# A decode kernel of two interleaved layers: two P buffers, half a V unit more kept on chip, and wq's space as ring slots

## The chip, the cores and the metric

The kernel runs on one core of a Trainium2 chip. The core has a matrix engine (TensorE, PE in the profile), a vector engine (VectorE, DVE), an activation engine (ScalarE, ACT), GpSimd (POOL, used for a little setup only) and SyncE (SP), which here does nothing but issue DMAs and wait. The engines run their own instruction streams in order and meet through semaphores. SBUF is the on-chip memory of 128 partitions, PSUM the accumulators that TensorE writes. The metric is the device time in microseconds (us), as the median of several runs; lower is better.

## The reference

Two rounds of the same pair of layers, on a batch of four rows with one token each. Both rounds use the same weights and the same K and V caches, so every cache byte that isn't kept on chip is read twice.

```
B, D, Hq, Hkv, Sk, Dh, F = 4, 512, 32, 8, 8192, 128, 1792
def A(x):                      # grouped-query attention on a cache
    q = (x @ wq) as (B, Hq, 1, Dh)           # 4 query heads share a K/V head
    p = softmax(q @ k_cache.T * Dh**-0.5)
    return (p @ v_cache) as (B, 1, Hq*Dh) @ wo
def Bf(x):                     # feed-forward network (FFN)
    return (silu(x @ w_gate) * (x @ w_up)) @ w_down
x = A_x
x = x + A(layernorm(x));  x = x + Bf(layernorm(x))      # "layer 0"
x = x + A(layernorm(x));  x = x + Bf(layernorm(x))      # "layer 1"
```

All tensors are bf16. K and V caches are 4 x 8 x 8192 x 128 each, 134 MB together, and the four rows are independent of each other up to the end.

## The kernel before, in words

**Units.** The caches are read in units of 4096 positions of one row `b` and one K/V head ("group" `g`): 1 MiB, 8 KB in each of 128 partitions. There are two units (`cp` 0 and 1) to a group, eight groups to a row, four rows, two layers `l`: 128 units of K and 128 of V. A unit lies in one of ten slots of a ring in SBUF (`pool`, `NSLOT`), each with a semaphore of its own; a unit has two halves of 2048 positions.

**K.** VectorE transposes both halves in place in 32 x 32 blocks (`k_pair`, L576, 1.2 us each). TensorE multiplies them with the padded query (L588) into four PSUM banks that hold the scores of a whole row. When all 16 units of a row have been added, `softmax` takes the maxima (L606), the exponentials into one of the buffers of `pp` (the "P buffer", L610), a common maximum for each query head (L620 to L649), and transposes P (L665, L671). A pass of a row is ready 18 to 22 us after its last K unit landed.

**V.** `v_group` multiplies P with the two units of a group (`pv4`, L744), folds the four column groups together on VectorE (L763, L766), turns the result (L772) and scales it into `oT` (L781). `oproj` (L707) multiplies a group's part of `oT` with wo; in layer 0 it follows each group of each row, and in layer 1 it follows the groups of row 3 alone, for all four rows at once. The very last V group of the order takes a direct form (`pv1`, L730) that needs no fold.

**Between the layers.** When all eight groups of a row are through layer 0, `chain` runs that row's FFN, a LayerNorm and the projection with wq (L465, in two halves), and only then can K of layer 1 of that row be multiplied. The rows are staggered: the passes (l, b) run in the order (0,0), (0,1), (1,0), (0,2), (1,1), (0,3), (1,2), (1,3). After (1,3) there is one more FFN for all rows (`ffn`), whose result is transposed back (`fin1`, L1023), copied (`fin2`, L1030) and stored (L1038).

**What stays on chip.** Of each row five V units (groups 0 and 1, and `cp` 0 of group 2) stay in their slots from layer 0 to layer 1 (`KEPT`, `kept_of`); the load is left out in layer 1 (`vload`). 128 + 108 units and the weights make 261.4 MB.

**What sets the order.** Loads are issued by SP alone, in the order of the string `ORDER`: a letter is a K unit, a V unit, or a piece of a weight (q, o, g, u, d for wq, wo, gate, up, down). K units come in the order of the passes, V units in that of `vgroups`. Everything else is placed by a planner (`Plan`): it knows a fixed time for each step, runs the steps on model engines, gives each load the slot that has been free longest (`pump`), picks at each point the ready step with the lowest priority number, and then the program is emitted in order of the planned starts. So the order on each engine, and which load goes into which slot, are fixed when the kernel is built. A V step's priority is the place of its load in `ORDER`; a unit that is kept takes the place of the load before it.

**What sets the waits.** `_Sync` keeps for every named piece of memory the last writer and the readers since. An instruction that reads a name waits for its last writer; one that writes a name waits for its last writer and all readers. For a DMA the writer's mark is its semaphore with all 16 signals, that is, its landing:

```
for w in writes:
    rec = self.res.get(w)
    if rec is not None:
        add(rec.w)
        for sv in rec.r.values():
            add(sv)
```

SP's waits (L62) stand in its queue, so what is behind a waiting load isn't issued. A load waits for the readers of its slot, which are TensorE's products with the unit before.

Of the kernel before, what the change touches and what calls it, by code (L numbers as in the profile page):

```python
# [102 lines left out]
class Step:  # L103
    __slots__ = ("eng", "us", "deps", "fn", "prio", "take", "free", "start", "end", "loads", "slot_of", "pairs")

    def __init__(self, eng, us, fn, deps, prio, take=None, free=None, pairs=0):
        self.eng, self.us, self.fn, self.prio = eng, us, fn, prio
        self.pairs = pairs
        self.deps = [d for d in deps if d is not None]
        self.take, self.free = take, free  # L110
        self.start = self.end = None
        self.slot_of = None


class Plan:
# [26 lines left out]
    def run(self):  # L142
# [44 lines left out]
        def pump(now):  # L187
            nonlocal li, sp_at, dma_at
            while li < len(self.loads):
                s = self.loads[li]  # L190
                t = sp_at
                if s.slot_of is not None:
                    if not slots:
                        return
                    slots.sort()
                    f, i = slots[0]
                    t = max(t, f)
                    if t > now:
                        return
                    slots.pop(0)  # L200
                    self.slot[s.slot_of] = i
                s.start = t
                sp_at = t + 0.4
                dma_at = max(dma_at, t + self.LOAD_LEAD) + s.us
                s.end = dma_at + self.LOAD_TAIL
                li += 1
                finish(s)
# [4 lines left out]
        while left:  # L212
# [16 lines left out]
            if li < len(self.loads) and (slots or self.loads[li].slot_of is None):  # L229
                nxt = max(sp_at, min(slots)[0] if self.loads[li].slot_of is not None else 0.0)  # L230
# [20 lines left out]
            if s.slot_of is not None:  # L251
                slots.append((s.end + self.HOP, self.slot[s.slot_of]))
            left -= 1
# [5 lines left out]
    def emit(self):  # L259
        for s in sorted(self.steps + self.loads, key=lambda s: (s.start, s.prio[0])):  # L260
# [3 lines left out]
ORDER = ("qKVKKKKKKKKVKKVVKKKKVgKKKKuKgKKKoVVVVVKKKVKKKVVKKKVVVuoododVKVKVKKKKVKKKKKKKVKKKVVVKVKKKKKKKKKKV"  # L264
         "KKKKKVVVVVVVVVVVVVVVVVVVKKVKKKKKKKKKVKKKKKKVVKKVVKKKKVKVKKKKVKKKKVVVVVVVVVVVVVVVVVVKKKKKKKKKKKKK"
         "KKKVVVVVVVVVVVVVVVVKVVVVKVKKKKKKKKKKKKKKVVVVVVVVVVVVVVV")
KEPT = [5, 5, 5, 5]
NSLOT = 10
VCUT = [4, 5, 0, 3]
NTAIL = [0, 3, 4, 1]  # L270


def bass_interleave_layers__gqa_block_cached__swiglu_ffn__decode_kernel(
# [33 lines left out]
    with ExitStack() as es:  # L307
# [7 lines left out]
        pp = sb("pp", [P, 3, NCH * 512], BF16)  # L315
# [8 lines left out]
        invL = sb("invL", [P, 3, 32], FP32)  # L324
        xrow = pp[0:B, 0, 0:D]
        ones1 = sb("ones1", [P, 1], FP32)
# [14 lines left out]
        negm = sb("negm", [P, 3, 4], FP32)  # L341
        lsum = sb("lsum", [P, 3, 4], FP32)
        gm = sb("gm", [P, 1], FP32)
        gl = sb("gl", [P, 1], FP32)
        alpha = sb("alpha", [P, 3, 4], FP32)
# [7 lines left out]
        xoT = sb("xoT", [P, NQ * B], BF16)  # L353
# [14 lines left out]
        sem_slot = [sem(f"sem_slot{i}") for i in range(NSLOT)]  # L368
        sem_x = sem("sem_x")
        sem_out = sem("sem_out")  # L370
# [67 lines left out]
        def layer_norm(dep, tag):  # L438
            m = col_sum(XT, mean, "x", "mean", [dep], tag + "m")

            def center():
                op("dve", lambda e: e.tensor_tensor(xnT[:].rearrange("p (n b) -> p n b", b=B), XT[:], over_nq(mean),
                                                    ALU.subtract), reads=["x", "mean"], writes=["xnT"])
                op("dve", lambda e: e.tensor_tensor(dT[:], XT[:], over_nq(mean), ALU.subtract),
                   reads=["x", "mean"], writes=["dT"])
                op("dve", lambda e: e.tensor_tensor(sqT[:], dT[:], dT[:], ALU.mult), reads=["dT"], writes=["sqT"])
            c = PL.add("dve", 0.5, center, [m], CHAIN)
            v = col_sum(sqT, var, "sqT", "var", [c], tag + "v")
# [97 lines left out]

        def unit_ap(u, h):
            s = PL.slot[home[u]]
            return pool[:, s, h * UE:(h + 1) * UE], f"slot{s}_{h}"

        def load_pair(u):
            kind, l, b, g, cp = u

            def fn():
                s = PL.slot[home[u]]
                cache = A_k_cache if kind == "k" else A_v_cache
                src = cache[b, g, cp * 2 * CR:(cp + 1) * 2 * CR, :].rearrange("(p t) d -> p (t d)", p=P)
                T.dma("sp", pool[:, s, :], src, sem_slot[s], writes=[f"slot{s}_0", f"slot{s}_1"])
            home[u] = u
            return PL.load(2.5, fn, u)  # L560
# [3 lines left out]
        p_free = {0: None, 1: None, 2: None}  # L564
# [150 lines left out]
        def v_group(l, b, g, lds, prios):  # L715
# [4 lines left out]
            for i, cp in enumerate(VCP):  # L720
# [32 lines left out]
                if not (l == 0 and (g, cp) in kept_of[b]):  # L753
                    st.slot_of = home[u]
                prev = st
# [19 lines left out]
            if not direct:  # L775
                prev = PL.add("dve", 0.9, fold, [prev], CHAIN)
# [13 lines left out]
        def ffn_mm(w_sb, wname, deps, tag):  # L790
            def fn():
                bk = pbk(tag)
                for fo in range(FO):
                    for kt in range(KT):
# [5 lines left out]
                           sig=(kt == KT - 1 and fo == FO - 1))  # L800
            return PL.add("pe", 1.65, fn, deps + [w_load[f"{wname}0"], w_load[f"{wname}1"]], CHAIN, take=tag, pairs=KT * FO)

        def ffn(dep, tag, dst=None, dkey="x"):
            v = lambda t: t.rearrange("p (f b) -> p f b", b=B)
            cen, root = layer_norm(dep, tag + "n")
            gate = ffn_mm(wg_sb, "wg", [cen], tag + "g")
            up = ffn_mm(wu_sb, "wu", [cen, gate], tag + "u")
# [9 lines left out]
            s = PL.add("act", 0.3, a2, [s], CHAIN)  # L817

            def a3():
# [3 lines left out]
                op("dve", lambda e: e.tensor_tensor(gs[:], gs[:], eneg[:], ALU.mult), reads=["gs", "eneg"], writes=["gs"])  # L823
            s = PL.add("dve", 1.0, a3, [s], CHAIN)

            def a4():
                bk = pbk(tag + "u")
                op("dve", lambda e: e.tensor_tensor(v(eneg[:]), v(ps[:, bk * BW:bk * BW + FO * B]), rstd_fo(), ALU.mult),
                   reads=[f"pb{bk}", "rstd"], writes=["eneg"])
                op("dve", lambda e: e.tensor_tensor(hT[:], gs[:], eneg[:], ALU.mult), reads=["gs", "eneg"], writes=["hT"])  # L830
            s = PL.add("dve", 0.45, a4, [s, up], CHAIN, free=tag + "u")
# [11 lines left out]
            return add_x(XT, "x", tag + "d", [s], dst, dkey)  # L843

        def add_x(base, key, tag, deps, dst=None, dkey="x"):
            to = XT[:].rearrange("p n b -> p (n b)") if dst is None else dst

            def fn():
                bk = pbk(tag) if tag else OPJ
                op("dve", lambda e: e.tensor_tensor(to, base[:].rearrange("p n b -> p (n b)"),  # L850
                                                    ps[:, bk * BW:bk * BW + NQ * B], ALU.add),
                   reads=[key, f"pb{bk}"], writes=[dkey])
            return PL.add("dve", 0.2, fn, deps, CHAIN, free=tag)

        def chain(b, deps, prior):
# [11 lines left out]
            q_ready[(1, b)] = out_  # L867

# [20 lines left out]
        def v_first(b):  # L889
            nk = -(-KEPT[b] // NCP)  # L890
            return [g for g in range(nk, G)] + list(range(nk))

        def v_second(b):
            nk = -(-KEPT[b] // NCP)
            kept, rest = list(range(nk)), list(range(nk, G))
            r = []
            while kept or rest:
                if kept:
                    r.append(kept.pop(0))
                if rest and (len(r) < 2 * nk - 2 or not kept):  # L900
                    r.append(rest.pop(0))
            return r
        vgroups = [(0, 0, g) for g in v_first(0)]
        rest = v_first(1)
        vgroups += [(0, 1, g) for g in rest[:G - NTAIL[1]]]
        for b in range(B):
            vgroups += [(1, b, g) for g in v_second(b)[:VCUT[b]]]
            if b + 1 < B:
                vgroups += [(0, b + 1, g) for g in v_first(b + 1)[G - NTAIL[b + 1]:]]
            vgroups += [(1, b, g) for g in v_second(b)[VCUT[b]:]]  # L910
            if b + 2 < B:
                vgroups += [(0, b + 2, g) for g in v_first(b + 2)[:G - NTAIL[b + 2]]]
# [36 lines left out]
        for i, (l, b) in enumerate(KSEQ):  # L949
            pb_of[(l, b)] = b % 3  # L950
# [47 lines left out]
        pend = list(vgroups)  # L998
# [19 lines left out]
        s = ffn(s, "z", dst=xoT[:], dkey="xo")  # L1018

        def fin1():  # L1020
            bk = pbk("out")
            for nq in range(NQ):
                op("pe", lambda e: e.matmul(bank_bf(bk)[0:B, nq * P:(nq + 1) * P], lhsT=xoT[:, nq * B:(nq + 1) * B],  # L1023
                                            rhs=ident[:], is_transpose=True, start=True, stop=True),
                   reads=["xo", "ident"], writes=[f"pb{bk}"], sig=(nq == NQ - 1))
        s = PL.add("pe", 0.6, fin1, [s], CHAIN, take="out", pairs=NQ)

        def fin2():
            bk = pbk("out")
            op("dve", lambda e: e.tensor_copy(xrow, bank_bf(bk)[0:B, 0:D]), reads=[f"pb{bk}"], writes=["xrow"])  # L1030
        PL.add("dve", 0.4, fin2, [s], CHAIN, free="out")
# [6 lines left out]
        nc.sync.dma_start(out.rearrange("b s d -> (b s) d"), xrow).then_inc(sem_out, 16)  # L1038
        nc.sync.wait_ge(sem_out, 16)

# [28 lines left out]
```

## Time and profile before

| | |
|---|---|
| median of 3 runs | 654.46 us (653.19 to 657.21) |
| the profiled execution: its own time | 656.26 us |
| its span, first to last instruction | 654.4 us |
| mean granted TensorE clock | 0.645 |
| TensorE busy | 473.6 us (72%) |
| VectorE busy | 461.6 us (71%) |
| ScalarE busy | 48.4 us (7%) |
| read from HBM | 261.36 MB, 399 GB/s over the span |
| chain that ended last | DMA 56%, TensorE 24%, VectorE 14%, SP 4%, issue 2% |

The profile is of one execution, and times in it count from the span's start. Busy time leaves out semaphore and DMA-issuing instructions. Its slices divide the span into 40 equal parts of 16.4 us. A "releaser" is what an engine's wait ended on. The landing of a load is when its semaphore has all 16 signals; the trace holds each signal. With the DMA queue full, two K units land 2.49 us apart.

The last load lands at 640.4. K's last unit of row 3, layer 1, lands at 602.9, its scores end at 608.3, and its P is ready at 620.8.

### The profile page before, as it was taken

Reading aid. Unit: us, or ns where it says so; the run is one execution under the profiler, and the core shown is the slowest. Engines: PE = TensorE matmul, PEld = TensorE weight load, DVE = VectorE, ACT = ScalarE, POOL = GpSimd, SP = SyncE. Lnnn points to the kernel's source line nnn. Section 1 sums busy time; section 2 is a strip of 40 time slices with the busy share of each in tenths; the row PEclk is TensorE's granted clock in tenths of the full one; section 3 lists DMA queues with packets and bytes.
Section 4 is the critical chain, followed back from the end, with each engine's and each line's share of the span. In section 5 each row is a group of like instructions: output and inputs, shape, how many; then the busy total and the mean of one; then the engine's idle time right before and its main releaser. Section 6 shows DMA issues by size and latency. Waiting matters only on the chain.

```text
span 654.4 us, 17105 instructions
## 1 busy us (share of the span) xinstructions
PE 473.6 (72%) x7774; PEld 208.7 (32%) x7774; DVE 461.6 (71%) x822; ACT 48.4 (7%) x114; POOL 2.7 (0%) x8
## 2 busy tenths in 40 slices
PE   2565457676876787677987686777877788977697
PEld 2211123125421232245422132235421234521246
DVE  2786684764697899744698888864699645689453
ACT  1000110003000110110000110030000200000300
POOL 1000000000000000000000000000000000000000
PEclk9975687665576578755555668755577665567655
DMA  8999999999999999999999999999999999999990
GB/s 350 419 422 407 402 398 419 420 416 393 408 416 412 412 419 420 420 419 417 378 426 418 421 419 421 420 420 419 391 389 422 420 420 420 383 394 422 420 413 21
DMA packets 41673, 262.48 MB, mean 401 GB/s; under 512 B 3960, under 2 KB 9856, under 8 KB 10880
## 3 DMA queue, kind: packets, MB, share of 16 engines
q1 hardware_dynamic: 41600, 261.38, 97.7%
q8 instruction: 61, 1.00, 0.6%
q14 instruction: 12, 0.10, 0.0%
HBM read 261.36 MB, written 0.00 MB: 399 GB/s over the span
## 4 chain that ended last, share of the span: by engine, by line
DMA 56%; PE 24%; DVE 14%; SPq 4%; issue 2%; ACT 0%; DVEq 0%
DMA pool<-in_A_k_cache_dram 33%; DMA pool<-in_A_v_cache_dram 19%; DVE pool L576 8%; PE ps L744 7%; PE ps L588 7%; SPq L92 4%; DVE red L766 3%; DMA wd_sb<-in_B_w_down_dram 3%; PE ps L772 2%; PE ps L465 2%; PE ps L795 2%; PE ps L707 1%; DVE red L763 1%; PE ps L837 1%; PE ps L427 1%
## 5 line engine op out<-in xcount | busy, mean ns | idle before, releaser
L576 DVE STREAM_TRANSPOSE pool<-pool 128x1024 uint32<-128x1024 uint32 x256 | 303.2, 1222 | 57.1 <-DMA pool<-in_A_k_cache_dram 50.1
L588 PE MATMUL ps<-pool,qpad 32*32 32x512 bf16 x4096 | 238.3, 541 | 74.4 <-DVE pool L576 69.4
L588 PEld LDWEIGHTS ps<-pool,qpad 32*32 32x32 bf16 x4096 | 67.6, 108 | 222.9 <-DVE pool L576 148.0
L744 PE MATMUL ps<-pool,pp 128*32 128x512 bf16 x1008 | 112.4, 556 | 30.9 <-DMA pool<-in_A_v_cache_dram 27.7
L766 DVE SCALAR_TENSOR_TENSOR red<-ps,mask,red 128x128 f32<-128x128 f32 x189 | 66.3, 351 | 6.7
L772 PE MATMUL ps<-sel,red 128*128 128x4 f32 x126 | 33.1, 337 | 41.2 <-DVE red L766 36.3
L763 DVE TENSOR_SCALAR red<-ps,mask 128x128 f32<-128x128 f32 x63 | 21.7, 344 | 54.5 <-PE ps L744 48.5
L772 PEld LDWEIGHTS ps<-sel,red 128*128 128x128 f32 x126 | 28.0, 279 | 76.0 <-DVE red L766 71.2
L610 ACT ACTIVATE pp<-ps,negm 128x512 bf16<-128x512 f32 x32 | 21.5, 685 | 408.4 <-DVE negm L606 408.4
L744 PEld LDWEIGHTS ps<-pool,pp 128*32 128x32 bf16 x1008 | 20.8, 109 | 72.4 <-DMA pool<-in_A_v_cache_dram 47.1
L707 PEld LDWEIGHTS ps<-oT,wo_sb 128*128 128x128 bf16 x640 | 20.6, 105 | 17.5 <-DVE oT L781 9.5
L606 DVE TENSOR_REDUCE negm<-ps 128x1 f32<-128x512 f32 x32 | 19.8, 680 | 8.5 <-PE ps L588 8.5
L707 PE MATMUL ps<-oT,wo_sb 128*128 128x4 bf16 x640 | 22.2, 167 | 3.9 <-DVE oT L781 3.8
L465 PE MATMUL ps<-xnT,wq_sb 128*128 128x4 bf16 x640 | 18.1, 166 | 7.8 <-DMA wq_sb<-in_A_wq_dram 7.3
L781 DVE TENSOR_TENSOR oT<-ps,invL 128x4 bf16<-128x4 f32 x64 | 9.9, 157 | 18.6 <-PE ps L772 17.8
L465 PEld LDWEIGHTS ps<-xnT,wq_sb 128*128 128x128 bf16 x640 | 18.1, 105 | 8.9 <-DMA wq_sb<-in_A_wq_dram 7.4
L665 PE MATMUL ps<-ident,pp 128*128 128x128 bf16 x128 | 15.7, 299 | 5.1 <-DVE pp L656 4.8
L671 ACT ACTIVATE pp<-ps 128x1024 bf16<-128x1024 bf16 x16 | 16.3, 1023 | 32.7 <-PE ps L665 32.7
L665 PEld LDWEIGHTS ps<-ident,pp 128*128 128x128 bf16 x128 | 12.0, 137 | 11.9 <-DVE pp L656 6.6
L451 ACT ACTIVATE lnv<-var,eps_sb 128x4 f32<-128x4 f32 x10 | 3.0, 296 | 117.9 <-DVE var L433 117.9
L837 PE MATMUL ps<-hT,wd_sb 128*128 128x4 bf16 x280 | 8.5, 166 | 4.0 <-DMA wd_sb<-in_B_w_down_dram 2.1
L837 PEld LDWEIGHTS ps<-hT,wd_sb 128*128 128x128 bf16 x280 | 8.0, 104 | 6.7 <-issue 3.5
(73 smaller groups left out, 154.8 us busy)
## 6 DMA issues: line engine op xcount, KB each, us to landing
pool<-in_A_k_cache_dram SPq DMA_DIRECT2D x128, 1024.0 KB, 9.4
pool<-in_A_v_cache_dram SPq DMA_DIRECT2D x108, 1024.0 KB, 11.8
wq_sb<-in_A_wq_dram SPq DMA_DIRECT2D x1, 4096.0 KB, 12.5
wo_sb<-in_A_wo_dram SPq DMA_DIRECT2D x4, 1024.0 KB, 14.9
wg_sb<-in_B_w_gate_dram SPq DMA_DIRECT2D x2, 896.0 KB, 20.7
wu_sb<-in_B_w_up_dram SPq DMA_DIRECT2D x2, 896.0 KB, 22.9
wd_sb<-in_B_w_down_dram SPq DMA_DIRECT2D x2, 896.0 KB, 19.3
pp<-in_A_x_dram SPq DMA_DIRECT2D x1, 4.0 KB
```

The costliest lines, as they stand in the source:

```text
L92: ins = self.eng[engname].dma_start(out_ap, in_ap)
L465: op("pe", lambda e: e.matmul(ps[:, bk * BW + h * B:bk * BW + (h + 1) * B], lhsT=wq_sb[:, kt, h * Dh:(h + 1) * Dh], rhs=xnT[:, kt * B:(kt ...
L576: op("dve", lambda e: e.transpose(v, v), reads=[key], writes=[key])
L588: op("pe", lambda e: e.matmul(ps[32 * c:32 * (c + 1), a * BW:(a + 1) * BW], lhsT=qpad[rows, qbuf, es_, g, :], rhs=ap[h][rows, :, es_ // 2, ...
L610: op("act", lambda e: e.activation(pblk(q)[:, :, a, :], bank(a).rearrange("p (t j) -> p t j", j=32), ACTF.Exp, bias=negm[:, q, a:a + 1], s ...
L665: op("pe", lambda e: e.matmul(stg[:, t * P:(t + 1) * P], lhsT=pp[:, q, blk * P:(blk + 1) * P], rhs=ident[:], is_transpose=True, start=True ...
L707: op("pe", lambda e: e.matmul(ps[:, OPJ * BW + nq * B:OPJ * BW + (nq + 1) * B], lhsT=wo_sb[:, h, nq * P:(nq + 1) * P], rhs=oT[:, l, h, :], ...
L744: op("pe", lambda e: e.matmul(ps[32 * j:32 * (j + 1), bk * BW:(bk + 1) * BW], lhsT=pp[:, q, at:at + 32], rhs=ap[:, 4 * j * Dh:4 * (j + 1) ...
L763: op("dve", lambda e: e.tensor_scalar(red[:], blk, mask4[:, t:t + 1], None, op0=ALU.mult), reads=[f"pb{bk}", "mask4"], writes=["red"])
L766: op("dve", lambda e: e.scalar_tensor_tensor(red[:], blk, mask4[:, t:t + 1], red[:], op0=ALU.mult, op1=ALU.add), reads=[f"pb{bk}", "mask4" ...
L772: op("pe", lambda e: e.matmul(ps[:, bk * BW:bk * BW + REP], lhsT=red[:], rhs=sel8[:, REP * (g % 2):REP * (g % 2 + 1)], start=True, stop=True),
L837: op("pe", lambda e: e.matmul(ps[:, bk * BW + nq * B:bk * BW + (nq + 1) * B], lhsT=wd_sb[:, fo, nq * P:(nq + 1) * P], rhs=hT[:, fo * B:(fo ...
```

## The change

- `pp` and the small tiles of the softmax have two buffers instead of three, by pass: `pb_of[(l, b)] = i % 2` where it was `b % 3`.
- A new tile `hold` of 4 KB in each partition takes the space of the third P buffer. It keeps the first half of one more V unit of the current row (`half_of`: group 2, `cp` 1). In layer 0 this unit is loaded by two DMAs, one into `hold` and one into the second half of a slot; in layer 1 only the second half is loaded. The load into `hold` for row b+1 is planned after layer 1 of row b has used it (`after`).
- The 32 KB per partition of `wq_sb` become four slots (numbers 10 to 13) of the ring once the last projection with wq, that of row 3, has run (`more`).
- The order of V groups is a list (`VGROUPS`: layer, row, group) instead of being built from rules; with it a new `ORDER`. The list ends with groups of row 2.
- The last FFN (`ffn_out`) puts the residual and the down product into PSUM with rows in partitions 0, 32, 64 and 96, through four column tiles, so that the transposes back are left out; four stores instead of one, from SP and ScalarE.
- In every FFN: the LayerNorm's subtraction is a step of its own ahead of the squares, the gate product is two steps, and the scale by `rstd` is done beside the exponential.

```diff
+                if s.after is not None:
+                    if s.after.end is None:
+                        return
+                    t = max(t, s.after.end + self.HOP)
...
+            for i in s.more:
+                slots.append((s.end + self.HOP, i))
...
-ORDER = ("qKVKKKKKKKKVKKVVKKKKVgKKKKuKgKKKoVVVVVKKKVKKKVVKKKVVVuoododVKVKVKKKKVKKKKKKKVKKKVVVKVKKKKKKKKKKV"
-         "KKKKKVVVVVVVVVVVVVVVVVVVKKVKKKKKKKKKVKKKKKKVVKKVVKKKKVKVKKKKVKKKKVVVVVVVVVVVVVVVVVVKKKKKKKKKKKKK"
-         "KKKVVVVVVVVVVVVVVVVKVVVVKVKKKKKKKKKKKKKKVVVVVVVVVVVVVVV")
+ORDER = ("qKKKKKKKKVKVKVoKKKKKKKVKVVVKuKVKKVKVKKKVKKKVVoKKVKVVoouddggVVVKKKKKKKKKKKKVKKKVKVVVVVKKKVKKKVVKK"
+         "KVKVVKKVKVVKVVVVKVKKKVVKKVVKKKVKKVKKKKKKKKVVVVKVVVKKVKKVKKKKKVVVVVKVVKVVKVVKKKVVVKVKVKKKKKKKKVVK"
+         "KKKKVVVVVVVVVVVVVVKVKVVVKKKKKKKKKKKKKKVVVVVVVVVVVVVVVVV")
...
-VCUT = [4, 5, 0, 3]
-NTAIL = [0, 3, 4, 1]
+VGROUPS = ("003 006 004 005 000 001 007 002 014 016 017 015 013 102 012 011 010 121 103 130 106 104 107 105 "
+           "111 024 027 023 026 021 100 131 112 020 101 022 025 117 115 113 116 114 035 033 037 034 122 031 "
+           "036 120 030 032 127 124 134 125 136 132 133 110 135 137 123 126")
...
-        pp = sb("pp", [P, 3, NCH * 512], BF16)
+        pp = sb("pp", [P, 2, NCH * 512], BF16)
+        hold = sb("hold", [P, UE], BF16)
...
-        sem_slot = [sem(f"sem_slot{i}") for i in range(NSLOT)]
+        sem_slot = [sem(f"sem_slot{i}") for i in range(NSLOT + KT)]
...
+        def slot_ap(s):
+            return pool[:, s, :] if s < NSLOT else wq_sb[:, s - NSLOT, :]
...
-                T.dma("sp", pool[:, s, :], src, sem_slot[s], writes=[f"slot{s}_0", f"slot{s}_1"])
+                if kind == "v" and half_of[b] == (g, cp):
+                    if l == 0:
+                        T.dma("sp", hold[:], src[:, 0:UE], sem_hold, writes=["hold"])
+                    T.dma("sp", slot_ap(s)[:, UE:2 * UE], src[:, UE:2 * UE], sem_slot[s],
+                          writes=[f"slot{s}_1"] + ([] if s < NSLOT else ["wq"]))
+                    return
+                T.dma("sp", slot_ap(s), src, sem_slot[s],
+                      writes=[f"slot{s}_0", f"slot{s}_1"] + ([] if s < NSLOT else ["wq"]))
...
+                if l == 1 and half_of[b] == (g, cp) and b + 1 < B:
+                    loads[("v", 0, b + 1) + half_of[b + 1]].after = st
...
-            gate = ffn_mm(wg_sb, "wg", [cen], tag + "g")
-            up = ffn_mm(wu_sb, "wu", [cen, gate], tag + "u")
+            gate = ffn_mm(wg_sb, "wg", [cen], tag + "g", range(4))
+            gate = ffn_mm(wg_sb, "wg", [gate], tag + "g", range(4, FO))
+            up = ffn_mm(wu_sb, "wu", [cen, gate], tag + "u", range(FO))
...
+        def ffn_out(dep, up, tag):
...
+            def res():
+                bk = pbk(n)
+                for nq in range(NQ):
+                    op("pe", lambda e: e.matmul(ps[32 * nq:32 * nq + B, bk * BW:bk * BW + P], lhsT=XT[:, nq, :],
+                                                rhs=identf[:], start=True, stop=False, tile_position=(0, 32 * nq)),
+                       reads=["x", "identf"], writes=[f"pb{bk}"], sig=(nq == NQ - 1))
...
+                    for nq in range(NQ):
+                        op("pe", lambda e: e.matmul(ps[32 * nq:32 * nq + B, bk * BW:bk * BW + P],
+                                                    lhsT=hT[:, fo * B:(fo + 1) * B],
+                                                    rhs=wd_sb[:, fo, nq * P:(nq + 1) * P],
+                                                    start=False, stop=(fo == FO - 1), tile_position=(0, 32 * nq)),
+                           reads=["hT", "wd0", "wd1"], writes=[f"pb{bk}"], sig=(fo == FO - 1 and nq == NQ - 1))
...
+            if b == B - 1:
+                mm.more = range(NSLOT, NSLOT + KT)
...
-            pb_of[(l, b)] = b % 3
+            pb_of[(l, b)] = i % 2
...
-        pend = list(vgroups)
+        pend = sorted(vgroups, key=lambda x: kpos[x[:2]])
```

## The prediction

> **What bounds the kernel now.** I read the page's slices first, then the queues, then what the SyncE queue (SP), which issues every load, waits for, then the times at which single loads land.
>
> ```profile
> DMA  8999999999999999999999999999999999999990
> GB/s 350 419 422 407 402 398 419 420 416 393 408 416 412 412 419 420 420 419 417 378 426 418 421 419 421 420 420 419 391 389 422 420 420 420 383 394 422 420 413 21
> q1 hardware_dynamic: 41600, 261.38, 97.7%
> ```
>
> One DMA queue moves 261.4 MB and is busy 97.7% of the span. 261.4 MB at the 420 GB/s of the undisturbed slices is 622 us of 654.4. The rest is a start (the first load, wq, is issued at 1.2 and lands at 13.6), dips, and a tail after the last load.
>
> ```profile
> SPq L62 <- PE ps L588: 270.7, 120, 7.8
> SPq L62 <- PE ps L744: 196.5, 81, 14.7
> ```
>
> SP spends 467 us waiting for TensorE to free a slot of the ring. While it waits nothing later is issued; that costs nothing as long as loads issued earlier are still queued. Each load signals its own semaphore. From the sixteenth signal of each I get its landing: with a full queue two 1.05 MB loads land 2.49 us apart, and issue to landing takes 8 us or more. Where issue to landing falls below 7.6 us the spacing often widens, because the queue ran dry. These excesses sum to 3.1 us, and 4.1 with one neighbour (landing at 583.05). I use 3.6. The dip is in the window table (busy time by engine, granted clock, DMA share, GB/s):
>
> ```profile
> 560.00:570.00 10.00, 9.54 (x216) 6.20 (x212) 6.88 (x19) 0.50 (x2) 0.00 (x0) 0.50 0.95 367
> 570.00:580.00 10.00, 7.38 (x151) 2.63 (x158) 9.45 (x13) 0.00 (x0) 0.00 (x0) 0.84 1.00 370
> 590.00:600.00 10.00, 6.89 (x128) 2.08 (x128) 9.56 (x9) 0.00 (x0) 0.00 (x0) 0.79 1.01 420
> ```
>
> This is row 3's layer-0 FFN and query projection: K of layer 1 waits for its query, the ring fills, SP stops. The last load lands at 640.4, and 14.0 us follow. The chain that ended last shows what they hold:
>
> ```profile
> 640.87 1.80 PE ps L730 x64
> 643.10 0.87 PE ps L707 x32
> 644.22 0.63 PE ps L427 x2
> 645.60 0.61 PE ps L427 x2
> 646.21 1.49 PE ps L795 x56
> 649.86 1.67 PE ps L837 x56
> 651.78 0.60 PE ps L1023 x4
> ```
>
> PV of the last V group, its projection, LayerNorm, gate and up, down, the transposes back. So the time is the DMA stream plus its holes plus that tail, and each part of the change is weighed by these three.
>
> **Bytes.** For each of four rows half a unit (2.10 MB in all) isn't read again: 2.10 MB / 420 GB/s = **-5.0 us**. Twelve loads become half loads with 4 KB rows, four of them additional. Nearest row: the weight loads with 3.5 KB rows land 2.26 us apart for 0.92 MB, 406 GB/s, so twelve halves lose 12 x 0.04 = +0.5; the other end is 0. I take **+0.3**. Four more issues of 0.33 us disappear in SP's 467 idle us. The Trainium skill (DMA: Bandwidth & Descriptors, "Anatomy of one DMA") fits a fixed 2.0 us to each DMA, on another issuing path; by it four added DMAs would cost 8 us, and the 2.49 us spacing here shows that a queued successor hides it.
>
> **The wait on `hold`.** Row b+1's half may be loaded only after layer 1 of row b has used it, and SP stands still until then. I laid the new order of loads out at 2.49 us per unit. The tightest place is row 1: K of layer 1, row 0 is complete at 214, its P follows 18 to 22 us later as before (232 to 236), the second half lands at 235 and is used by 236 to 240. The `hold` load is due at 247, so must be issued by 243. Margin 3 us or more: 0. Row 3 has 4 us, row 2 over 20. If the cover went, each us late is a us of stream.
>
> **Two P buffers.** The exponentials of a pass now wait for all PV of the pass two earlier. In the new order the last V of that pass lands 28 to 51 us before the K that would need the buffer: 0.
>
> **The new order.** The V groups that a query projection waits for now land 30 us ahead of layer 1's K in rows 1 and 2 (26 and 23 before), so the dips around 320 and 480 should go. Row 3 keeps its gap: its last layer-0 V lands at 539.3, the projection ended 24 us after that landing before, so about 563. Between -4.1 (all holes filled) and +4.1 (as many again elsewhere) I take **-3.6**, and price row 3's hole by itself: five slots hold kept V, five hold K without a query, the sixth K (layer 1, row 3, group 5) is due at 564.6, is issued at 563 and lands at 568: **+3.0**.
>
> **The four wq slots.** Every load into one of them names "wq" among its writes besides its slot. The dependency tracker (`_need`) makes a writer wait for the last writer of each name it writes. After the first such load, that last writer is the previous load into a wq slot, and its semaphore says "landed". So SP waits for one load to land before it issues the next into a wq slot. The waiter is at SP's head: all later loads stand behind it. If other loads were issued between the two, the queue goes on; if the two are consecutive it is empty. The trace of before has no such wait. The price is issue to landing with nothing in front, less 2.49: wq lands 12.5 us after its issue, and its 4.19 MB take 9.97, which leaves 2.5. The shortest K load (issued 567.97) took 5.3, with its predecessor landing 2.85 after its issue, so at most 2.85. With the wake-up 2.6 to 3.0: **2.8 us a wait**.
>
> The wq load, by its tile:
>
> ```profile
> DMA to landing us min/median/max: 12.5/12.5/12.5
> ```
>
> The ring's loads, 560 to 583:
>
> ```profile
> DMA to landing us min/median/max: 5.3/8.9/9.9
> ```
>
> By the skill's fit, same section, it would be 2.0 us.
>
> How many are consecutive? All four slots enter the ring in the same instant, and the planner gives a load the slot that has been free longest, so the first four loads after the projection take them in a row: 3 waits behind the first. They come free in the same order, nothing between, since only K of one row is in work: after five loads into other slots the next four fall on them again, 3 more. Then K's slots come free one after another and two consecutive V loads take two of them (1), and near the end, when P is ready and the first two V are used, two more (1). 8 x 2.8 = **+22.4**.
>
> **The tail.** The stream now ends with groups 3 and 6 of row 2. No dependency leads from them to row 3's projection or to the last FFN; the planner may write that projection ahead of them, and then their part is not in it. What binds is TensorE's in-order queue: in the plan these PV fall into the gaps of row 3's last group, ahead of the gate product, so the gate stands behind the last landing. After it: one PV unit (1.0), then from gate to end. That stretch took 654.4 - 645.1 = 9.3 us. Removed: one multiply with its hop (0.25), the residual add with its hop (0.22), transposes (0.60); the gate's first part runs beside the variance (0.15) and the copy has 128 columns instead of 512 (0.1). Added: a second DMA issue (0.33), and the down projection, which moves 128 columns through four column tiles: PV's eight 512-column products side by side take 1.04 us, so 14 sets of 128 take 1.8 against 1.65. One after another it would be 56 x 0.13 = 7.3, the upper end; the L744 row is the nearest in form. Net -0.8: 8.5, so tail 9.5 instead of 14.0: **-4.5**.
>
> **Sum,** on the profiled execution: 654.4 - 5.0 + 0.3 - 3.6 + 3.0 + 22.4 - 4.5 = **667.0** of span. That execution's own time was 656.3, 1.9 above its span, while the median of the three runs, 654.46, equals the span, so I carry the difference of 12.6 to the median: **667**.
>
> **Rivals.**
> 1. *The waits never empty the queue* (faster): if other loads always stand between two wq loads, a wait passes while 2.49 us or more are queued. Then 667.0 - 22.4 = **644.6**. For it: the other terms are a real gain. Against it: four slots that appear together. With k consecutive pairs the time is 644.6 + 2.8k, so it decides at k = 3.5. That the extra slots do nothing at all ends near here too (647), as the ring stalls for row 3 as before.
> 2. *The first round alone counts* (k = 2 to 5; later slots interleave with V's): 650 to 659, mostly no change.
> 3. *The last two V groups come after the FFN's products* in TensorE's order: the program then ends 2 to 6 us after the last landing instead of 9.5, that is 660 to 664. This lies inside the forecast.
>
> **How the numbers follow.** Forecast 0.68, own range 656 (six waits at 2.6 and the late-PV order) to 673 (nine at 3.1); rival 2 0.12; rival 1 0.20. Measurements of this kernel tell about 1% (6.5 us). Faster is rival 1: 0.20. Within 1% are most of rival 2 and the low end of the forecast: 0.18. Slower: 0.62. The range reaches from 646, which takes in rival 2 and the slow half of rival 1, to 672.
>
> **What would show it.** Right: after about 563 us SP waits for pool's DMAs, by 2 us and more each; landings 5.2 to 5.4 us apart in two runs of three; GB/s near 200 in slices around 570 to 585 and 600 to 615; last landing near 657; K of the last row complete near 603 although it was planned 13 us earlier; before 540 dips fewer than now. Wrong: SP waits for TensorE alone after 563 and the stream stays at 420. A dip near 240 would mean that `hold` binds; a down projection of 7 us, that the column tiles run one after another.

## The result, and the profile after

The changed kernel takes 672.3 us (median of three, 671.6 to 672.8) against 655.25 us for the kernel before, measured beside it: ratio 1.0249, 95% interval 1.0215 to 1.0284. It is 17 us slower; the forecast was 667, 12.6 slower. A second set of runs (e1 below) gave 671.87 us and 1.0251 (1.0228 to 1.0274). A fourth execution, the profiled one, ran at a granted clock of 0.292 and took 1113.6 us, so it is in none of these numbers, and all lines of "after" here are e1's: the same kernel, span 671.6 us, its own time 673.44 us.

The slices and queues of the page after:

```profile
DMA  8999999999999999999999999999999997687891
GB/s 354 420 406 420 409 421 420 404 401 396 408 419 407 422 418 419 421 407 360 424 421 399 421 420 418 420 409 394 422 420 420 420 419 286 246 337 274 320 418 69
q1 hardware_dynamic: 42184, 259.28, 95.0%
q8 instruction: 61, 1.00, 0.6%
```

2.1 MB fewer are read, as meant, and up to the 33rd slice (about 554 us) the stream is nearly as dense as before. Then five slices fall to 246 to 337 GB/s. The window table has the place (columns: window and its length; busy us and number of instructions of TensorE, its weight loads, VectorE, ScalarE and GpSimd; granted clock, DMA share, GB/s):

```profile
560.00:570.00 10.00, 8.06 (x217) 5.51 (x222) 8.96 (x17) 0.50 (x2) 0.00 (x0) 0.50 0.79 292
570.00:580.00 10.00, 6.98 (x170) 2.98 (x154) 4.75 (x5) 0.00 (x0) 0.00 (x0) 0.84 0.56 206
580.00:590.00 10.00, 4.58 (x65) 1.23 (x65) 6.17 (x6) 0.00 (x0) 0.00 (x0) 0.50 0.79 318
590.00:600.00 10.00, 6.50 (x113) 1.83 (x112) 8.22 (x8) 0.00 (x0) 0.00 (x0) 0.66 1.01 421
600.00:610.00 10.00, 6.17 (x96) 1.51 (x80) 6.58 (x6) 0.00 (x0) 0.00 (x0) 0.51 0.38 141
```

From 570 to 610 TensorE and VectorE are less busy there than before, so nothing suggests that an engine has become the bound. What SP waited for (us in total, times, longest) says what has:

```profile
SPq L62 <- PE ps L619: 230.1, 99, 8.2
SPq L62 <- PE ps L775: 164.0, 78, 6.8
SPq L62 <- DMA wq_sb<-in_A_v_cache_dram: 40.5, 5, 18.2
...
SPq L62 <- DMA wq_sb<-in_A_k_cache_dram: 22.9, 3, 15.8
SPq L92 <- DMA wq_sb<-in_A_k_cache_dram: 15.3, 3, 6.2
```

The first two are the old waits for a slot. The last three are new: eleven waits of SP for a landing in wq's space, one for each load there but the first. SP's own timeline shows what they do to the order of issue (start, us, what, how many):

```profile
564.88 16.70 SPq L92 DMA_DIRECT2D wq_sb<-in_A_k_cache_dram  x4
581.68 2.56 SPq L92 DMA_DIRECT2D pool<-in_A_k_cache_dram  x5
586.15 16.52 SPq L92 DMA_DIRECT2D wq_sb<-in_A_k_cache_dram  x2
608.06 5.24 SPq L92 DMA_DIRECT2D wq_sb<-in_A_v_cache_dram  x2
613.39 2.57 SPq L92 DMA_DIRECT2D pool<-in_A_v_cache_dram  x5
```

Five loads into the ring are issued in 2.6 us; four loads into wq's space take 16.7. The groups alternate as the forecast counted them, four and five. The chain that ended last runs through nine of the twelve loads into wq's space (start, us, what):

```profile
564.88 6.54 DMA wq_sb<-in_A_k_cache_dram
571.44 4.86 DMA wq_sb<-in_A_k_cache_dram
576.31 4.93 DMA wq_sb<-in_A_k_cache_dram
581.26 4.82 DMA wq_sb<-in_A_k_cache_dram
586.15 16.12 DMA wq_sb<-in_A_k_cache_dram
602.34 5.65 DMA wq_sb<-in_A_k_cache_dram
...
638.05 18.57 DMA wq_sb<-in_A_v_cache_dram
656.68 4.77 DMA wq_sb<-in_A_v_cache_dram
...
661.50 1.01 PE ps L761 x32
662.51 0.46 PE ps L444 x2
...
663.43 0.59 PE ps L828 x16
...
667.54 1.58 PE ps L899 x29
669.15 0.29 DVE pp L907
```

Each DMA link is one load from its issue to its landing. Most take 4.8 to 4.9 us, where 2.49 would be the share of a load in a full queue; 16.1 and 18.6 are loads with five or more others ahead, 6.5 is one with another load ahead, and 5.65 is one of the late loads of which e9 tells. The last load lands at 661.45, and TensorE is at that moment waiting for it with the last PV (L761), ahead of the FFN's products.

The emitted order confirms one more thing that the prediction left open: the projections of groups 3 and 6 in layer 1 stand ahead of row 2's scaling of these groups, so these two groups of row 2 are not in the last projection of the changed kernel. The trace agrees: in e1 the last projection is added to the residual at 658.6, and the last scaling follows at 662.5. So the changed kernel does a little less than the kernel before. What that is worth in time is e7.

### The profile page after: what moved, and what is told of

Its sections match the earlier page's. It is cut to its first block, busy times and chain, and to the rows that moved or that the text cites. A ratio compares the mean times of both kernels' runs of the same rounds, so it can differ in the third digit from the quotient of the medians.

```text
span 1111.8 us, 17106 instructions
## 1 busy us (share of the span) xinstructions
PE 1008.0 (91%) x7778; PEld 414.9 (37%) x7778; DVE 461.1 (41%) x821; ACT 48.5 (4%) x114; POOL 2.7 (0%) x8
## 4 chain that ended last, share of the span: by engine, by line
PE 77%; DMA 18%; DVE 3%; SPq 2%; issue 0%; ACT 0%
PE ps L619 33%; PE ps L775 22%; DMA pool<-in_A_k_cache_dram 10%; DMA pool<-in_A_v_cache_dram 6%; PE ps L805 5%; PE ps L828 3%; PE ps L484 3%; PE ps L738 3%; PE ps L696 2%; PE ps L444 2%; SPq L92 2%; DVE pool L607 2%; DMA wd_sb<-in_B_w_down_dram 2%; PE ps L877 1%; PE ps L670 1%; PE ps L720 1%
## 5 line engine op out<-in xcount | busy, mean ns | idle before, releaser
L619 PE MATMUL ps<-pool,qpad 32*32 32x512 bf16 x3904 | 437.7, 1105 | 39.3 <-DVE pool L607 37.0
L775 PE MATMUL ps<-pool,pp 128*32 128x512 bf16 x944 | 252.8, 1264 | 20.8 <-DMA pool<-in_A_v_cache_dram 19.4
L619 PEld LDWEIGHTS ps<-pool,qpad 32*32 32x32 bf16 x3904 | 97.8, 175 | 331.2 <-issue 239.6
L805 PEld LDWEIGHTS ps<-sel,red 128*128 128x128 f32 x126 | 66.4, 694 | 111.0 <-issue 83.2
L805 PE MATMUL ps<-sel,red 128*128 128x4 f32 x126 | 69.1, 619 | 10.0 <-DVE red L799 9.7
L738 PEld LDWEIGHTS ps<-oT,wo_sb 128*128 128x128 bf16 x640 | 48.6, 176 | 20.8 <-issue 8.2
L738 PE MATMUL ps<-oT,wo_sb 128*128 128x4 bf16 x640 | 43.8, 200 | 6.4 <-DVE oT L814 3.5
L484 PEld LDWEIGHTS ps<-xnT,wq_sb 128*128 128x128 bf16 x640 | 40.8, 170 | 13.9 <-DMA wq_sb<-in_A_wq_dram 7.4
L619 PE MATMUL ps<-wq_sb,qpad 32*32 32x512 bf16 x192 | 28.6, 1646 | 0.0
L828 PEld LDWEIGHTS ps<-xnT,wg_sb 128*128 128x128 bf16 x280 | 22.7, 193 | 6.6 <-issue 5.5
```

The costliest lines, as they stand in the source:

```text
L484: op("pe", lambda e: e.matmul(ps[:, bk * BW + h * B:bk * BW + (h + 1) * B], lhsT=wq_sb[:, kt, h * Dh:(h + 1) * Dh], rhs=xnT[:, kt * B:(kt ...
L619: op("pe", lambda e: e.matmul(ps[32 * c:32 * (c + 1), a * BW:(a + 1) * BW], lhsT=qpad[rows, qbuf, es_, g, :], rhs=ap[h][rows, :, es_ // 2, ...
L738: op("pe", lambda e: e.matmul(ps[:, OPJ * BW + nq * B:OPJ * BW + (nq + 1) * B], lhsT=wo_sb[:, h, nq * P:(nq + 1) * P], rhs=oT[:, l, h, :], ...
L775: op("pe", lambda e: e.matmul(ps[32 * j:32 * (j + 1), bk * BW:(bk + 1) * BW], lhsT=pp[:, q, at:at + 32], rhs=ap[:, 4 * j * Dh:4 * (j + 1) ...
L805: op("pe", lambda e: e.matmul(ps[:, bk * BW:bk * BW + REP], lhsT=red[:], rhs=sel8[:, REP * (g % 2):REP * (g % 2 + 1)], start=True, stop=True),
L828: op("pe", lambda e: e.matmul(ps[:, bk * BW + fo * B:bk * BW + (fo + 1) * B], lhsT=w_sb[:, kt, fo * P:(fo + 1) * P], rhs=xnT[:, kt * B:(kt ...
```

## The experiments

All times are medians, beside runs of the kernel before on the same chip; e1 to e4 ran on one chip (before: 655.74), e5 to e8 on another (655.66), e9 and e10 on a third (655.18).

### e1: the changed kernel once more

> The changed kernel as it is, for a profile beside the others. Theory (SP waits for the landing of the load before, eight times with an empty queue): about 672 us; after the projection with wq at about 563 us, eight pairs of landings about 4.9 to 5.3 us apart, the last landing near 660. Rival (another part of the change holds the stream back, the wait on hold or the new order): pairs 2.5 us apart after 563 and the holes before it. As in the changed kernel, row 2's V groups 3 and 6 of layer 1 come too late for the last projection and are not in it; this holds for e2 to e4 as well.

Measured: 671.87 us. The theory's pairs are there, and they are eight: the landings that follow a load in wq's space with nothing queued behind it come 4.88, 4.94, 4.83, 5.72, 4.91, 4.82, 4.91 and 4.83 us after it. Above the spacing of 2.48 this is 20.0 us. The rival's spacing of 2.5 is not there.

### e2: a name for each wq slot

```diff
-  writes=[f"slot{s}_0", f"slot{s}_1"] + ([] if s < NSLOT else ["wq"]))
+  writes=[f"slot{s}_0", f"slot{s}_1"] + ([] if s < NSLOT else [f"wq{s - NSLOT}"]))
...
-  reads=["wq", "xnT"], ...
+  reads=["wq0", "wq1", "wq2", "wq3", "xnT"], ...
```

The load of wq itself writes all four names, so that each slot still waits for the projection, but not for another slot's load. Plan, order and slots are unchanged.

> Each wq slot has a dependency name of its own, so that a load into it no longer waits for the load into another one; plan and order are unchanged. Theory: eight waits of 2.4 to 2.8 us go, 672 becomes 650 to 653. Rival (waits don't matter, another part costs the time): 668 to 672. If it comes out at 645 the forecast's other terms were right too.

Measured: **650.12 us**, ratio 0.9920 (0.9901 to 0.9938). 21.75 us less than e1: the waits are the loss, and without them the change, still without two groups of row 2 in its last projection, is 0.8% faster than the kernel before. It is not the 645 that would have confirmed the forecast's other terms: they were 4 to 5 us too good. In SP's waits the lines for a landing in wq's space are gone (the third line is the wait for the result at the end):

```profile
SPq L62 <- PE ps L620: 259.1, 113, 8.2
SPq L62 <- PE ps L776: 172.3, 78, 6.8
SPq L1076 <- DVE pp L908: 28.3, 1, 28.3
```

The same windows of e2 as of e1 above:

```profile
570.00:580.00 10.00, 6.80 (x107) 1.70 (x97) 8.81 (x8) 0.00 (x0) 0.00 (x0) 0.71 1.00 417
...
600.00:610.00 10.00, 5.32 (x44) 2.90 (x37) 6.39 (x18) 4.06 (x11) 0.00 (x0) 0.50 1.01 420
```

417 instead of 206 GB/s, and 420 instead of 141. Issue to landing of the loads of wq's space, first in e1:

```profile
DMA to landing us min/median/max: 4.7/4.9/18.6
```

and in e2:

```profile
DMA to landing us min/median/max: 6.4/16.7/20.7
```

The single load got slower and the kernel faster: 16.7 us is a load that waits its turn in a full queue, 4.9 one that had the queue to itself.

### e3: two names in turns

```diff
+ [f"wq{(s - NSLOT) % 2}"]
```

> Two names for the four slots, in turns: a load into a wq slot waits for the landing of the one before the previous one, with one load in the queue between them. Theory (only an empty queue costs): as e2 within 2 us, 650 to 655. Rival (every such wait costs its 2.4 to 2.8 us, whatever is queued): about eight waits less two, 664 to 668.

Measured: 652.70 us, 0.9969 (0.9950 to 0.9989), as the theory has it. SP still waits for landings in wq's space, eight times, 30 us in total:

```profile
SPq L62 <- DMA wq_sb<-in_A_k_cache_dram: 18.3, 3, 15.1
...
SPq L92 <- DMA wq_sb<-in_A_k_cache_dram: 7.7, 2, 4.1
...
SPq L62 <- DMA wq_sb<-in_A_v_cache_dram: 4.0, 3, 2.1
```

They cost 2.6 us against e2 (3.2 by the ratios), 0.3 to 0.4 each, with one load queued behind the one that is waited for. So what costs is not the wait but the queue that is empty when it ends. Part of the 2.6 us shows at one place: the first load after K of the last row lands 3.63 us after its predecessor instead of 2.48. Most of the rest is in three later loads, 0.4 to 0.5 us each.

### e9: two names in pairs

```diff
+ [f"wq{(s - NSLOT) // 2}"]
```

> Two names for the four wq slots, one for slots 10 and 11 and one for 12 and 13: of the eight waits with an empty queue six stay (10 to 11 and 12 to 13 in the first two rounds, 10 to 11 in the third, 12 to 13 at the end). Theory (2.4 us for each): e2's 650.1 + 6 x 2.4 = 664.5, 663 to 666. Rival (what counts is the longest chain of waits in a row, now one instead of three): about a third of e1's excess, 657. Row 2's V groups 3 and 6 of layer 1 aren't in the last projection, as in e2.

Measured: 668.96 us, 1.0213 (1.0194 to 1.0232): above both expectations. The rival falls clearly. The theory's six pairs are in the landings, and they measure 15.3 us above the spacing, near the expected 14.4; but 18.8 us are lost against e2 (medians on two chips; 19.6 between the two spans). The rest is in neither theory: between the waits some loads land late although others are queued before and behind them, by 1.26, 0.63, 1.40, 0.46 and 0.89 us. In e1 there are five such loads too, 4.3 us in all; in e2 no spacing after 582 us is above 2.50.

The trace holds a candidate. The page's q8 is the fetching of instructions: 61 packets of 16 KB, and 0.6% of sixteen engines' span is 1.05 us for each. After 582 us, e1 has such packets at 594.8, 603.1, 631.0, 640.2 and 655.3 before its last landing. Loads land late at 597.3, 608.0, 633.1 and 641.1 to 644.2, by 1.34, 0.8 (in the pair of 5.72), 1.09 and 1.28 us; the fifth packet shows no loss, nor do two earlier ones among the first waits (570.4 and 575.9), and one late load (0.55 us, at 629.5, the half unit) has no packet beside it. e2 has its five packets after 582 too, at 587.1 to 634.3, with no loss.

The sixteen signals of each load show how. In e1's restarted stream they come close together: those of the load that lands at 593.5 within 0.59 us. Of the next load, beside the packet at 594.8, fifteen come within 0.59 us again and one 1.91 us after the first; the landing is that one. At 633.1 it is the same, fifteen within 0.78 and one at 1.93, and in e9 at 594.2, fifteen within 0.56 and one at 1.80, beside a packet at 591.6. In e2's long full stream the signals of a load are spread over 3.0 to 3.1 us. Around its packet at 587.1 one of them falls back from 0.29 to 1.8 us behind the first, and the last stays at 3.1, so the landing doesn't move. This fits a fetch that holds up one share of sixteen: it shows in full where the shares are level, and not where another share is later still. e4 fits too: its queue ran empty before the landing at 621.46, and it has a packet at 628.1 and a load 1.2 us late at 630.3. What stays open: the trace doesn't say which of the sixteen engines carries a packet or a signal, and no run takes the fetches away. That the packets are the cause rests on their coincidence in time with one late signal; it is argued, not tested.

### e4: without the four slots

```diff
-            if b == B - 1:
-                mm.more = range(NSLOT, NSLOT + KT)
```

> The change without the four extra slots; planned anew with ten slots and the same order of loads. Theory: no landing waits, but row 3's hole grows by 2 to 5 us against e2: 650 to 658. Rival (the new order or hold is what makes the change slow): 665 or more.

Measured: 654.69 us, 0.9986 (0.9970 to 1.0003). The rival falls: with ten slots alone the new order is no slower than the kernel before. Against e2 the four slots are worth 4.6 us when their loads don't wait for each other. In the stream, e2's hole at row 3's query projection holds 4.8 us, e4's 8.9, and e4 loses 2.4 more just before P of row 3 is ready (landing 621.46), where the ring is full of V.

### e5 and e6: the half unit, and the P buffers

```diff
- half_of = {b: (KEPT[b] // NCP, KEPT[b] % NCP) for b in range(B)}
+ half_of = {b: None for b in range(B)}                 # e5 and e6
- pb_of[(l, b)] = i % 2
+ pb_of[(l, b)] = i % 3                                  # e6 alone, with three buffers
```

> e2 (a name for each wq slot) without hold: the half unit is read again in layer 1, 2.10 MB more; planned anew, same order. Theory (bytes at the stream's rate): 5.0 us more than e2's 650.1, 654 to 656. Rival (the half loads and the wait on hold eat up part of the bytes): 650 to 653. Row 2's V groups 3 and 6 of layer 1 aren't in the last projection, as in e2.

> e5 with three P buffers, taken in turns. Theory (the waits for a P buffer are covered by 28 us or more): as e5 within 1.5 us. Rival (two buffers delay the exponentials and with them the ring): 2 us or more below e5. Row 2's V groups 3 and 6 of layer 1 aren't in the last projection, as in e2.

Measured: e5 654.20 us (0.9976, 0.9961 to 0.9991), e6 653.81 us (0.9969, 0.9950 to 0.9988). The half units are worth 3.7 us by the ratios and 4.1 by the medians, against 5.0 by their bytes; each of the two intervals is about 1.1 us to either side, so 5.0 is not excluded, and neither is that half loads lose a part of it. A third P buffer gives 0.4 us, less than these runs can tell from nothing.

### e7 and e8: all rows in the last projection, and the hole

```diff
- wdep = [...] if l == 0 else []
+ wdep = [...] if l == 0 else [ndone[(1, r, g)] for r in range(B - 1)]      # e7 and e8
...
- "... 127 124 134 125 136 ..."       and ORDER's ...KVKVVVKKKK, 17 V at the end
+ "... 127 124 125 134 136 ..."       and ORDER's ...KVKVVVVVKKKK, 15 V at the end   # e8
```

> e2 with the projection of each group in layer 1 waiting for that group of all four rows, so that all of layer 1 is in the last projection. Theory: scale, projection of one group and residual come behind the last landing, 0.2 + 0.6 + 0.2 and hops, 1 to 2 us above e2: 651 to 652. Rival (the planner keeps several projections back and the tail grows by more): 653 or more.

> e7 with the two units of row 2's group 5 loaded ahead of K's third unit of row 3 instead of after K, to fill the hole of the stream at 556 to 573 (4.8 us in e2). Theory: the hole shrinks to 1 to 2 us and the end comes 1 to 3 us earlier than in e7: 648 to 651. Rival (P of row 3 and the products behind it set the end, not the stream): as e7 or later.

Measured: e7 **650.75 us**, 0.9922 (0.9902 to 0.9941); e8 650.65 us, 0.9924 (0.9907 to 0.9941). The complete projection costs 0.1 us by the ratios and 0.6 by the medians. From e7's last landing (638.7) to the end of its span are 11.4 us instead of e2's 10.1, with the last projection (0.60) and the residual in them; e7's own stream took 1.7 us longer than e2's. So with all rows in the last projection, as before the change, e7 is 0.8% faster than the kernel before; nothing that was run is faster than e2, e7, e8 and e10 by more than the runs can tell.

e8 changes nothing in the medians, as its rival has it. In its trace the hole is 4.0 us in all against 5.5 in e7 and 4.8 in e2, not 1 to 2: 3.98, 3.97 and 3.11 us before the landings at 562.74, 569.35 and 574.93, the first of these now a V unit that was issued only 6.0 us ahead. Its stream ends 2.7 us earlier than e7's (636.0), and from its last landing to its end are 12.0 us, 0.6 more than in e7, with three projections behind the last PV. So between these two traces 2.1 us are left, but e8's is its fastest execution and e7's its slowest; the medians, 0.1 us apart, show no gain, and why not stays open. In e7's chain the softmax of row 3 and the products behind it set the end from 605 on; in e8's it is the last load again, from its issue at 618.7 to 636.0.

### e10: the old last down product

e7 with the down product, residual, transposes, copy and single store of before.

> e7 with the last down product, residual, transposes back, copy and single store as before the change; the parted gate and the rest of the FFN stay. Theory: the transposes and the residual add with their hops (0.8) and the longer copy come back, one store instead of two issued in a row on SP goes (0.3): 0.5 to 1 us above e7's 650.75. Rival (the new tail gives nothing or costs): at or below 650.75.

Measured: 650.68 us, 0.9930 (0.9914 to 0.9946), with e7 at 650.75: the rival, no gain. The traces say why. The end of e10's chain:

```profile
644.36 1.67 PE ps L879 x56
...
646.05 0.18 DVE xoT L919
...
646.28 0.60 PE ps L1073 x4
...
646.90 0.41 DVE pp L1080
```

From the gate's start (640.36) to the end of the copy are 6.95 us; in e1, from 663.43 to 669.44, they are 6.01, and in e7 as well. So the form without transposes does save 0.94. But with its four stores, two from SP and two from ScalarE, it is 2.1 us from the copy to the end of the span, and 1.6 with the single store. The net 0.4 us is below what the runs can tell.

## Why the prediction was right, and where it was off

**The direction and the mechanism held.** The step that carried the forecast was that a load into wq's space waits, at SP's head, for the landing of the previous one, and that this empties the queue. e2 takes the name away and the loss with it; e3 keeps the waits but not the empty queue and loses 2.6 us of 21.75. The slots fell as forecast, in runs of four, five, four, and the eight pairs came where they were counted. Of the other signs, the windows near 200 GB/s came (206 at 570 to 580, 141 at 600 to 610); the pairs were closer than forecast (4.8 to 4.9 instead of 5.2 to 5.4), K of the last row was complete at 608 instead of 603, the last landing was at 661 instead of 657, and the dips before 540 were not fewer. Rival 1, the waits that never empty the queue, is e2 and e3 in measured form: 650 to 653, not the case here. Rival 2 falls with the count. Rival 3 did not occur: the last PV stands ahead of the FFN in TensorE's order.

**The sizes.** On the spans, forecast 667.0, measured 671.6. By terms:

| term | forecast | measured | from |
|---|---|---|---|
| price of eight waits | 22.4 | 20.0 | e1's landings, 2.34 to 3.24 each |
| late loads between them | none | 4.3 | e1's landings |
| order of loads, with the hole at row 3 | -0.6 | +2.1 | loss against the bytes at 420.5 GB/s: 18.85 at before's last landing, 20.95 in e1 at 571.4 |
| half units: bytes and form | -4.7 | -5.0 | the bytes; by time, e5 against e2, -3.7 to -4.1 |
| last landing to the end | -4.5 | -3.9 | 10.1 against 14.0 |

The measured terms give 654.4 + 20.0 + 4.3 + 2.1 - 5.0 - 3.9 = 671.9 of span, 0.3 from e1's. That the total is only 4.6 off is in part luck: the waits were put 2.4 too high and the half units 0.3, while the late loads, the order and the tail together were put 7.6 too low.

The price was too high: I took 2.8 from a wq load of 2.5 beyond its transfer and a K load of at most 2.85, and added a wake-up (0.01 to 0.09 us from landing to the next issue in e1). About 2.35 is what a load of 1.05 MB needs beyond its 2.49 us with nothing in front; the 3.24 holds a late signal. The Trainium skill's fit (DMA: Bandwidth & Descriptors, "Anatomy of one DMA"), a fixed 2.0 us for another issuing path, with its rate would give an estimate of 4.4 us for such a load by itself; the traces show 4.7 to 4.9 here, between that and my 5.3.

The order was the term with the wrong sign. I let the dips of before go because the query projections of rows 1 and 2 had more room. By before's landings little was to be had there: of the 4.1 us, 1.3 lie at 326 to 487 and 2.8 at row 3. And in e1 there are others at 310 to 346, and at the last V of row 3's layer 0 (landing 542.35) e1's stream has lost 16.8 us against its bytes, where before's had lost 15.8 at the same load. The hole at row 3 cost 4.1 us instead of the forecast 3.0.

Hidden as forecast: the P buffers (e6), the wait on `hold` (no dip near 240 in e1), the column tiles of the last down product, 1.58 us against 1.8. The stretch of 9.3 us that the forecast calls "from gate to end" begins at the normalised input (xnT, 645.1 before); it was to shrink to 8.5 and came to 8.4. What the tail's term left out stands ahead of it: the LayerNorm's mean (L444 and L450, 0.65 us) comes behind the last PV as well, so that it is 1.75 us from the last landing to xnT instead of 1.0. Of the shorter FFN, the part in the down product alone is worth nothing that the runs can tell, since its gain goes into the stores (e10).

**The chances.** 0.62 for slower was on the right side. The measured median lies 5.3 us above the forecast. Taken as a plain time, 672.3 is 0.3 above the end of the stated range, 672; by its ratio, 1.0249 times the 654.46 from which the forecast started, it is 670.8, just inside. The late loads between the waits were in no term, and the order had the wrong sign.

## What to carry to other kernels

When memory is lent to a new use, give each piece a dependency name of its own: a shared name makes loads that have nothing to do with each other follow one another, and a load that waits for a landing costs little as long as another is queued behind that landing (0.3 us a wait in e3), and if none is, what issue to landing takes beyond the load's share of the stream (here 2.35 us for a load of 1.05 MB). Read it from the spacing of landings, not from a load's own time, which was 16.7 us where the kernel was fast and 4.9 where it was slow. And count what a list of loads releases in one instant: slots that come free together are used together, so a fault between two of them repeats.

## What was unexpected in the hardware

In a stream that is restarted from an empty queue, loads land late by 0.5 to 1.4 us, in e1 after 582 in four of five cases where an instruction packet (16 KB, 1.05 us) falls; in e2, whose queue did not run empty after 582, five such packets moved no landing by more than 0.02 us. In e9 such late loads come to 4.6 us beside the 15.3 us of its six waits. The difference shows in the sixteen signals of a load: within 0.5 to 1.0 us of each other after e1's waits, over 3.0 to 3.1 us in e2's full stream, where one signal falling back didn't move the landing.
